# Decode attention with a Mish MLP: keys transposed by VectorE instead of TensorE, query and probabilities exchanged with keys and values as matmul operands, one load queue

## The chip, the cores and the metric

One core of one Trainium2 chip. A core has TensorE (matrix products from SBUF into PSUM), VectorE, ScalarE and GpSimd (element-wise work), SP (here it only issues DMAs), and 16 DMA engines between HBM and SBUF. SBUF and PSUM have 128 partitions. A matmul takes two operands: the *fixed* one (`lhsT`, up to 128x128) is loaded into the array by LDWEIGHTS, the *moving* one (`rhs`, up to 512 columns) is then streamed through. The metric is device time in microseconds (us), here the median of three runs: 239.27 us (238.69 to 239.35).

## The reference

One token for each of two batch rows goes through attention over a window of a key/value cache and, beside it, through a small MLP. With `x` of shape (2, 1, 448), 16 query heads, 8 key/value heads, head size 256 and a window of 4096 keys:

```
xn = layernorm(x)
q  = xn @ wq                                   # wq 448 x 4096, 16 heads of 256
k, v = k_cache[:, :, -4096:, :], v_cache[:, :, -4096:, :]   # (2, 8, 4096, 256), each for 2 query heads
p  = softmax(q . k / 16)                       # over 4096 keys
A  = (p . v) @ wo                              # wo 4096 x 448
h  = xn @ w1 + b1;  B = (h * tanh(softplus(h))) @ w2        # 448 -> 1792 -> 448
out = x + A + B
```

All arrays are bfloat16. The windows of the cache are 2 x 16 x 2 MB, 67.1 MB; wq and wo are 3.67 MB each, w1 and w2 1.61 MB each.

## The kernel before, in words

There are 16 *heads* in the loop: 8 key/value heads (`kvh`) times 2 batch rows (`b`). A head has 4096 keys, put on the partitions as 128 x 32: partition p holds keys 32p to 32p+31, in T = 32 blocks `t` of 128 keys, one key of each partition in a block.

For each `kvh` SP loads a slice of wq (lines 200 and 207) and of wo (line 213), and TensorE makes the transposed query `qT` (line 223). For each head SP loads the keys in two DMAs of 1 MB (`Kn`, line 241), and ScalarE's queue the values in two (`Vt`, line 245); each has three buffers of a whole head. Then:

- **Transposes** (`emit_transposes`): TensorE transposes a key block of 128x128 with the identity as moving operand (line 255, 64 per head), 8 blocks into one PSUM tile; VectorE copies five of the eight to SBUF (line 261), ScalarE three (line 265).
- **Scores** (`emit_scores`): each transposed block `KT` is loaded as the fixed operand and two columns, the two query heads, are streamed (line 274, 64 pairs of a load and a matmul per head). They run one group of 8 blocks behind the transposes.
- **Values**: ScalarE takes the exponential (line 289, 64 elements), VectorE the sums (line 292); then 32 matmuls with the probabilities (2 columns) as fixed operand and 256 value columns moving (line 301), a matmul for the denominators (line 308), the division (lines 316, 318), a transposition of the 2x256 result (lines 327, 332).
- After both batch rows of a `kvh`, four matmuls of 448 columns with wo add to `psA` (line 340).

The MLP's weights are loaded after `kvh` 1 (lines 98 to 105), and it is computed after `kvh` 3 (lines 149 to 189). At the end two additions (lines 354, 356) and the output DMA (line 357). Each engine runs its instructions in the order in which a scheduler has put them; the engines meet by semaphores. A DMA also waits for the one eight places before it, whose semaphore it reuses.

Of the kernel before, what the change touches and what calls it, by code (L numbers as in the profile page):

```python
# [12 lines left out]
FP32 = mybir.dt.float32  # L13


@with_exitstack
def kernel(
# [14 lines left out]
    P = 128  # L32

# [29 lines left out]
    wq_pool = ctx.enter_context(tc.tile_pool(name="wq", bufs=2))
    wo_pool = ctx.enter_context(tc.tile_pool(name="wo", bufs=2))
    qpool = ctx.enter_context(tc.tile_pool(name="q", bufs=2))
    kn_pool = ctx.enter_context(tc.tile_pool(name="kn", bufs=3))
    kt_pool = ctx.enter_context(tc.tile_pool(name="kt", bufs=2))
    v_pool = ctx.enter_context(tc.tile_pool(name="vv", bufs=3))
    pt_pool = ctx.enter_context(tc.tile_pool(name="pt", bufs=2))
    small = ctx.enter_context(tc.tile_pool(name="small", bufs=2))  # L70
    wmlp = ctx.enter_context(tc.tile_pool(name="wmlp", bufs=1))
    psum_tr = ctx.enter_context(tc.tile_pool(name="ps_tr", bufs=2, space=bass.MemoryType.PSUM))
    psum_sc = ctx.enter_context(tc.tile_pool(name="ps_sc", bufs=1, space=bass.MemoryType.PSUM))
    psum_po = ctx.enter_context(tc.tile_pool(name="ps_po", bufs=1, space=bass.MemoryType.PSUM))
    psum_ot = ctx.enter_context(tc.tile_pool(name="ps_ot", bufs=1, space=bass.MemoryType.PSUM))
    psum_mlp = ctx.enter_context(tc.tile_pool(name="ps_mlp", bufs=1, space=bass.MemoryType.PSUM))

    x_bf = consts.tile([Bsz, D], BF16)
    nc.sync.dma_start(out=x_bf[:, :], in_=A_x.flatten_outer_dims())

    ident = consts.tile([P, P], BF16)
    make_identity(nc, ident[:])

# [3 lines left out]
    ones1 = consts.tile([1, Bsz], BF16)  # L87
    nc.vector.memset(ones1[:], 1.0)

    ones_col = consts.tile([P, 1], FP32)  # L90
    nc.vector.memset(ones_col[:], 1.0)

    w1_sb = wmlp.tile([P, NJ, F], BF16)
    b1_sb = wmlp.tile([1, F], BF16)
    w2_sb = wmlp.tile([P, NFC, D], BF16)

    def emit_mlp_weight_dmas():
        nc.sync.dma_start(
            out=w1_sb[:, 0:nfull, :],
            in_=B_w1[0 : nfull * P, :].rearrange("(j p) n -> p j n", p=P),  # L100
        )
        if rem:
            nc.sync.dma_start(out=w1_sb[0:rem, nfull, :], in_=B_w1[nfull * P : D, :])
        nc.sync.dma_start(out=b1_sb[0:1, :], in_=B_b1.rearrange("(o f) -> o f", o=1))
        nc.sync.dma_start(
            out=w2_sb[:, :, :],
            in_=B_w2.rearrange("(c p) d -> p c d", p=P),
        )
# [18 lines left out]
    )  # L127

    xnT_ps = psum_misc.tile([P, NJ, Bsz], BF16, tag="pre")
    for j in range(NJ):  # L130
        csz = min(P, D - j * P)
        nc.tensor.transpose(  # L132
            xnT_ps[0:csz, j, :],
            xn_bf[0:Bsz, j * P : j * P + csz],
            ident[0:Bsz, 0:Bsz],
        )
    xnT_sb = consts.tile([P, NJ, Bsz], BF16)
    nc.vector.tensor_copy(out=xnT_sb[:, 0:nfull, :], in_=xnT_ps[:, 0:nfull, :])
# [3 lines left out]
    bsb = consts.tile([Bsz, D], FP32)

    def emit_mlp():
        hT_ps = psum_mlp.tile([P, NFC, Bsz], FP32, tag="m")
        for c in range(NFC):
            for j in range(NJ):
                ksz = min(P, D - j * P)
                nc.tensor.matmul(  # L149
                    hT_ps[:, c, :],  # L150
                    lhsT=w1_sb[0:ksz, j, c * P : (c + 1) * P],
                    rhs=xnT_sb[0:ksz, j, :],
                    start=(j == 0),
                    stop=False,
                )
            nc.tensor.matmul(  # L156
                hT_ps[:, c, :],
                lhsT=b1_sb[0:1, c * P : (c + 1) * P],
                rhs=ones1[0:1, 0:Bsz],
                start=False,  # L160
                stop=True,
            )
        h_sb = wmlp.tile([P, NFC, Bsz], FP32)
        nc.vector.tensor_copy(out=h_sb[:], in_=hT_ps[:])
        u_sb = wmlp.tile([P, NFC, Bsz], FP32)
        nc.scalar.activation(out=u_sb[:], in_=h_sb[:], func=ACT.Exp)
        v_sb = wmlp.tile([P, NFC, Bsz], FP32)
# [220 lines left out]
```

## Time and profile before

| | |
|---|---|
| median of three runs | 239.27 us |
| span of the profiled execution | 239.0 us |
| TensorE matmuls (PE), share of the span | 82%, 2872 instructions |
| TensorE weight loads (PEld) | 67% |
| VectorE (DVE) / ScalarE (ACT) | 33% / 28% |
| moved by DMA | 78.07 MB, 327 GB/s over the span |

The profiled execution is one run; its span, from the first to the last instruction, is 0.3 us short of the median time. PE and PEld overlap, and matmuls are pipelined: their busy time says that TensorE is at work, not that it is at its peak. In the chain of work that ended last TensorE has 57% of the span, DMA 20%, VectorE 11% and ScalarE 7%. The granted TensorE clock has two levels, 1.2 and 2.4 GHz; the profile gives it as a share of 2.4.

### The profile page before, as it was taken

To read this page: it belongs to the slowest core of one execution; us is meant where nothing else is said; L and a number is where in the kernel's file an instruction comes from. 1 tells how busy PE (TensorE), PEld (TensorE's weight loads), DVE (VectorE), ACT (ScalarE), POOL (GpSimd) and SP (SyncE) were. 2 spreads that over 40 slices of the span, in tenths; PEclk is the share of its full clock that TensorE was granted. 3 is DMA by queue.
4 is the path that set the end of the run, shared out by engine and by line. 5 is a ranking of instruction groups with operands and counts; after the bars stand their busy time and mean duration, and the time that the engine had idled before them with its cause. 6 is when DMAs were issued, how large, how long until landed. Compare 5 with 4: busy or idle time off the path is not lost.

```text
span 239.0 us, 6327 instructions
## 1 busy us (share of the span) xinstructions
PE 196.0 (82%) x2872; PEld 159.1 (67%) x2872; DVE 79.0 (33%) x217; ACT 67.2 (28%) x149; POOL 0.7 (0%) x6
## 2 busy tenths in 40 slices
PE   0228039949999999899989998999899989999892
PEld 0127037746797687778877877777777767777751
DVE  2003012411224253335333624352434334342603
ACT  2003104311113142315232523251425133432500
POOL 1000000000000000000000000000000000000000
PEclk9999999956857999999999999999999999999979
DMA  6999999999997999999999999999999999500000
GB/s 226 389 422 417 405 380 420 374 331 348 391 395 254 357 365 363 337 373 418 415 366 379 420 415 394 401 387 395 381 402 362 387 334 421 234 1 3 3 0 0
DMA packets 19605, 78.07 MB, mean 327 GB/s; under 512 B 1461, under 2 KB 10937, under 8 KB 11386
## 3 DMA queue, kind: packets, MB, share of 16 engines
q1 hardware_dynamic: 14970, 44.12, 48.9%
q10 hardware_dynamic: 4608, 33.56, 37.0%
q8 instruction: 22, 0.36, 0.6%
q14 instruction: 5, 0.04, 0.0%
HBM read 77.67 MB, written 0.00 MB: 325 GB/s over the span
## 4 chain that ended last, share of the span: by engine, by line
PE 57%; DMA 20%; DVE 11%; ACT 7%; issue 2%; SPq 1%; ACTq 0%
PE po L301 24%; PE pst L255 18%; DVE KT L261 9%; DMA wq_k<-in_A_wq_dram 7%; DMA w_sb<-in_B_w_dram 7%; ACT KT L265 7%; DMA Kn<-in_A_k_cache_dram 6%; PE psc L274 5%; PE psA L340 3%; PE qT_ps L223 3%; PE hT_ps L149 2%; DVE o_bf L318 1%; PE psB L182 1%; ACT pT L289 1%; PE hT_ps L156 1%
## 5 line engine op out<-in xcount | busy, mean ns | idle before, releaser
L265 ACT COPY KT<-pst 128x384 bf16<-128x384 bf16 x128 | 60.8, 478 | 150.6 <-DVE KT L261 117.5
L255 PE MATMUL pst<-ident,Kn 128*128 128x128 bf16 x1024 | 83.9, 233 | 9.9 <-DMA Kn<-in_A_k_cache_dram 5.6
L261 DVE COPY KT<-pst 128x640 bf16<-128x640 bf16 x128 | 61.8, 488 | 78.0 <-PE pst L255 76.1
L255 PEld LDWEIGHTS <-Kn 128*128 128x128 bf16 x1024 | 66.6, 104 | 11.0 <-DMA Kn<-in_A_k_cache_dram 5.7
L301 PE MATMUL po<-Vt,pT 128*2 128x256 bf16 x512 | 62.2, 283 | 1.1 <-ACT pT L289 0.7
L301 PEld LDWEIGHTS <-pT 128*2 128x2 bf16 x512 | 43.2, 87 | 17.7 <-ACT pT L289 2.4
L274 PE MATMUL psc<-qT_k,KT 128*128 128x2 bf16 x1024 | 49.5, 165 | 5.9 <-DVE KT L261 4.9
L274 PEld LDWEIGHTS <-KT 128*128 128x128 bf16 x1024 | 40.1, 98 | 16.7 <-DVE KT L261 10.2
L223 PE MATMUL qT_ps<-xnT_sb,wq_k 128*128 128x2 bf16 (+1 forms) x128 | 10.3, 170 | 14.3 <-DMA wq_k<-in_A_wq_dram 14.3
L316 DVE RECIPROCAL rec<-po 2x1 f32<-2x1 f32 x16 | 2.5, 155 | 57.1 <-PE po L308 57.1
L223 PEld LDWEIGHTS <-wq_k 128*128 128x128 bf16 (+1 forms) x128 | 8.3, 99 | 15.5 <-DMA wq_k<-in_A_wq_dram 14.6
L149 PE MATMUL hT_ps<-xnT_sb,w_sb 128*128 128x2 bf16 (+1 forms) x56 | 5.0, 172 | 3.5 <-DMA w_sb<-in_B_w_dram 3.5
L318 DVE TENSOR_SCALAR o_bf<-po,rec 2x256 bf16<-2x256 f32 x16 | 7.5, 471 | 0.5
L340 PE MATMUL psA<-wo_k,oT_k 128*2 128x448 bf16 x32 | 7.5, 355 | 0.3 <-DVE oT_k L332 0.3
L149 PEld LDWEIGHTS <-w_sb 128*128 128x128 bf16 (+1 forms) x56 | 3.5, 101 | 4.0 <-DMA w_sb<-in_B_w_dram 3.5
L289 ACT ACTIVATE pT<-psc 128x64 bf16<-128x64 f32 x16 | 3.6, 226 | 8.6 <-PE psc L274 4.7
L231 DVE CAST qT_k<-qT_ps 128x8 bf16<-128x8 f32 x8 | 1.3, 167 | 9.4 <-PE qT_ps L223 8.0
L292 DVE TENSOR_REDUCE red<-pT 128x2 f32<-128x64 bf16 x16 | 3.4, 210 | 2.3 <-ACT pT L289 2.3
L327 PE MATMUL oT_ps<-ident,o_bf 2*128 2x2 bf16 x32 | 3.2, 166 | 0.8 <-DVE o_bf L318 0.8
L132 PE MATMUL xnT_ps<-ident,xn_bf 2*128 2x2 bf16 (+1 forms) x4 | 0.4, 178 | 3.9 <-DVE xn_bf L120 3.9
L327 PEld LDWEIGHTS <-o_bf 2*128 2x128 bf16 x32 | 1.7, 92 | 2.7 <-DVE o_bf L318 0.9
L182 PE MATMUL psB<-w_sb,act_bf 128*2 128x448 bf16 x14 | 3.5, 352 | 0.0
(36 smaller groups left out, 23.8 us busy)
## 6 DMA issues: line engine op xcount, KB each, us to landing
Vt<-in_A_v_cache_dram ACTq DMA_DIRECT2D x32, 1024.0 KB, 7.8
Kn<-in_A_k_cache_dram SPq DMA_DIRECT2D x32, 1024.0 KB, 8.8
wo_k<-in_A_wo_dram SPq DMA_DIRECT2D x8, 448.0 KB, 9.2
wq_k<-in_A_wq_dram SPq DMA_DIRECT2D x8, 384.0 KB, 8.5
w_sb<-in_B_w_dram SPq DMA_DIRECT2D x1, 1568.0 KB, 20.4
w_sb<-in_B_w_dram SPq DMA_DIRECT2D x1, 1344.0 KB, 16.2
wq_k<-in_A_wq_dram SPq DMA_DIRECT2D x8, 64.0 KB, 8.3
w_sb<-in_B_w_dram SPq DMA_DIRECT2D x1, 224.0 KB, 17.0
```

The costliest lines, as they stand in the source:

```text
L149: nc.tensor.matmul(hT_ps[:, c, :], lhsT=w1_sb[0:ksz, j, c * P : (c + 1) * P], rhs=xnT_sb[0:ksz, j, :], start=(j == 0), stop=False,)
L182: nc.tensor.matmul(psB[:, :], lhsT=act_bf[:, c, :], rhs=w2_sb[:, c, :], start=(c == 0), stop=(c == NFC - 1),)
L223: nc.tensor.matmul(qT_ps[:, hl, dh, :], lhsT=wq_k[0:ksz, j, col0 : col0 + P], rhs=xnT_sb[0:ksz, j, :], start=(j == 0), stop=(j == NJ - 1),)
L255: nc.tensor.transpose(pst[:, tt, :], Kn[:, t, dh * P : (dh + 1) * P], ident[:],)
L261: nc.vector.tensor_copy(out=KT[:, dh, base : base + CSPLIT * P], in_=pst[:, 0:CSPLIT, :],)
L265: nc.scalar.copy(out=KT[:, dh, base + CSPLIT * P : base + GRP * P], in_=pst[:, CSPLIT:GRP, :],)
L274: nc.tensor.matmul(psc[:, t, :], lhsT=KT[:, dh, t * P : (t + 1) * P], rhs=qT_k[:, :, dh, b], start=(dh == 0), stop=(dh == NDH - 1),)
L289: nc.scalar.activation(out=pT[:], in_=psc[:], func=ACT.Exp, scale=scale)
L301: nc.tensor.matmul(po[:, 0:Dh], lhsT=pT[:, t, :], rhs=Vt[:, t, :], start=(t == 0), stop=(t == T - 1),)
L318: nc.vector.tensor_scalar(out=o_bf[:], in0=po[:, 0:Dh], scalar1=rec[:], scalar2=None, op0=ALU.mult,)
L327: nc.tensor.transpose(oT_ps[:, dh * rep : (dh + 1) * rep], o_bf[0:rep, dh * P : (dh + 1) * P], ident[0:rep, 0:rep],)
L340: nc.tensor.matmul(psA[:, :], lhsT=oT_k[:, :, col], rhs=wo_k[:, c, :], start=(kvh == 0 and hl == 0 and dh == 0), stop=(kvh == Hkv - 1 and ...
```

## The change

It is a new kernel for the same computation. A head is now worked on in two *steps* of 16 key blocks (`NH` = 2, 32 steps in all).

- **Loads.** All large loads are issued by SP in one order: the whole wq in two DMAs, then keys and values step by step, wo after the second batch row, w1 and w2 at step 3. wq and w1 lie on 112 partitions with four rows each, so that what a partition reads is 4 KB or more. Keys and values have six buffers each of half a head.
- **Keys** (`scores`): VectorE transposes the key tile in 32x32 blocks, with pairs of bf16 taken as one fp32 element (`kt`, 2048 elements a partition). A transposed tile then holds 32 elements of a key's head dimension on each 32 partitions, pairs side by side.
- **Scores**: the query is the fixed operand, block-diagonal over the four groups of 32 partitions (`qdiag`, eight matrices a head, written by GpSimd in `build_q`), and 512 columns of keys are moving, every second element (`ktv`); eight matmuls a step.
- **Probabilities**: ScalarE's exponential writes 512 columns and sums them as it goes; VectorE transposes them back in 32x32 blocks (`pT`).
- **Values** (`values`): a 128x128 block of values is the fixed operand (every second element of 256, `vv`), two columns of probabilities are moving; 32 pairs a step. The result is already transposed, so the transposition at the end of a head goes.
- wq is projected in two groups (`project`), the MLP in `dense_in` and `dense_out`; there is one addition at the end instead of two.

```diff
+    k_pool = ctx.enter_context(tc.tile_pool(name="kk", bufs=6))
+    v_pool = ctx.enter_context(tc.tile_pool(name="vv", bufs=6))
     kt_pool = ctx.enter_context(tc.tile_pool(name="kt", bufs=2))
+    p_pool = ctx.enter_context(tc.tile_pool(name="pp", bufs=2))
...
+        nc.sync.dma_start(
+            out=wq_sb[:, :, g * GW : (g + 1) * GW], in_=wq_in[:, :, g * GW : (g + 1) * GW]
+        )
...
+    def build_q(i):
+        kvh, b = heads[i]
+        t = qdiag[i % NW]
+        tv = t[:].rearrange("p (n e) c -> p n e c", e=NE)
+        for j in range(NQ):
+            rows = slice(j * Q, (j + 1) * Q)
+            for e in range(NE):
+                nc.gpsimd.tensor_copy(
+                    out=tv[rows, :, e, j * Q : j * Q + rep],
+                    in_=qrep[rows, :, kvh * rep : (kvh + 1) * rep, e, b],
+                )
...
+    def scores(s):
+        i = s // NH
+        kt = kt_pool.tile([P, TH * Dh], BF16, tag="kt", name="kt")
+        nc.vector.transpose(out=kt[:].bitcast(FP32), in_=k_t.pop(s)[:].bitcast(FP32))
+        ktv = kt[:].rearrange("p (t n c e) -> p n e t c", t=TH, n=NB, e=NE)
+        psc = ps_sc.tile([P, TH, Q], FP32, tag="sc", name="sc")
+        for n in range(NB):
+            for e in range(NE):
+                nc.tensor.matmul(
+                    psc[:],
+                    lhsT=qdiag[i % NW][:, n * NE + e, :],
+                    rhs=ktv[:, n, e, :, :],
...
+        nc.scalar.activation(
+            out=p_sb[:],
+            in_=psc[:].rearrange("p t c -> p (t c)"),
+            func=ACT.Exp,
+            scale=scale,
+            accum_out=state["rs", i][:, s % NH : s % NH + 1],
+        )
...
+    def values(s):
...
+        nc.vector.transpose(out=pT[:], in_=p_t.pop(s)[:])
...
+        vv = v[:].rearrange("p t (m c) -> p t c m", c=ND)
+        for t in range(TH):
+            for c in range(ND):
+                nc.tensor.matmul(
+                    po[:, c, :],
+                    lhsT=vv[:, t, c, :],
+                    rhs=pTv[:, t, 0:rep],
...
+        nc.vector.reciprocal(out=rec[:], in_=den[:])
...
+        nc.vector.tensor_tensor(
+            out=oT[:, :, :, b],
+            in0=po[:],
+            in1=rec[:].unsqueeze(1).to_broadcast([P, ND, rep]),
+            op=ALU.mult,
+        )
...
+    for s in range(NSTEP + 1):
+        if s + 2 < NSTEP:
+            load_k(s + 2)
+        if s + 1 < NSTEP:
+            load_v(s + 1)
...
+        if s < NSTEP:
+            scores(s)
+        if s >= 1:
+            values(s - 1)
```

VectorE before, in the second half of the program: a head's copies of the transposed keys (`KT<-pst`), the sum, the division and the small copy of the head before between them.

```order
L261 COPY KT_2243<-pst_2245 128x640 [waits PE_49]
L292 TENSOR_REDUCE red_2193<-pT_2191 128x2 [waits Activation_49]
L316 RECIPROCAL rec_2229<-po_2195 2x1 [waits PE_49]
L318 TENSOR_SCALAR o_bf_2231<-po_2195,rec_2229 2x256 [waits DVE_49]
L261 COPY KT_2243<-pst_2256 128x640 [waits PE_49]
L332 COPY oT_k_2030<-oT_ps_2233 128x4 [waits PE_49]
L261 COPY KT_2243<-pst_2267 128x640
```

VectorE after, at the same place: from the division of one head (`oT` from `o`) to that of the next. `kt<-k` is the transposition of a key tile, `pT<-p` that of the probabilities.

```order
L333 TENSOR_TENSOR oT_2008<-o_1908,rec_2006 128x4 [waits DVE_49,PE_49]
L299 STREAM_TRANSPOSE pT_2027<-p_1966 128x512 [waits Activation_49]
L271 STREAM_TRANSPOSE kt_2014<-k_1889 128x2048 [waits DMAHW1_49]
L271 STREAM_TRANSPOSE kt_2074<-k_1941 128x2048 [waits DMAHW3_49]
L299 STREAM_TRANSPOSE pT_2088<-p_2025 128x512 [waits Activation_49]
L329 RECIPROCAL rec_2125<-den_2122 128x2 [waits PE_49]
L333 TENSOR_TENSOR oT_2008<-o_2029,rec_2125 128x4 [waits DVE_49,PE_49]
```

The short copies that followed TensorE's transposes are gone. Two whole key tiles stand in a row, and the division of a head stands ahead of the next head's first `pT`.

TensorE after, at the same place: the denominator (`den`) behind the first value stage of a head, the scores of the next head (`sc_2076`), then the second value stage (`o_2029`, with 31 more pairs where the dots are), wo, and the scores of the step after.

```order
L321 MATMUL den_2122<-hsel_124,rs_1967 128x2 [waits Activation_49]
L276 LDWEIGHTS qdiag2_133 [waits DVE_49,Pool_49]
L276 MATMUL sc_2076<-kt_2074,qdiag2_133 128x512 [waits PE_49]
...
L308 LDWEIGHTS v_1943 [waits DMAHW4_49]
L308 MATMUL o_2029<-pT_2088,v_1943 128x2 [waits DVE_49]
...
L344 LDWEIGHTS oT_2008 [waits DVE_49]
...
L321 MATMUL den_2236<-hsel_124,rs_2086 128x2 [waits Activation_49]
L276 LDWEIGHTS qdiag2_133 [waits DVE_49]
L276 MATMUL sc_2138<-kt_2136,qdiag2_133 128x512 [waits PE_49]
```

A step's scores stand one step ahead of its values, and each waits for VectorE: the scores for `kt`, the values for `pT`.

## Rows read from the trace of the kernel before

**Rows 1.** The page: span, busy time, granted clock and GB/s in 40 slices.

```profile
span 239.0 us, 6327 instructions
...
PE 196.0 (82%) x2872; PEld 159.1 (67%) x2872; DVE 79.0 (33%) x217; ACT 67.2 (28%) x149; POOL 0.7 (0%) x6
...
PEclk9999999956857999999999999999999999999979
...
GB/s 226 389 422 417 405 380 420 374 331 348 391 395 254 357 365 363 337 373 418 415 366 379 420 415 394 401 387 395 381 402 362 387 334 421 234 1 3 3 0 0
```

**Rows 2.** Busy time by stretch: us, engines, granted clock, DMA share, GB/s.

```profile
0.00:6.00 6.00, 0.37 (x4) 0.28 (x4) 1.67 (x9) 1.58 (x2) 0.70 (x6) 1.00 0.70 226
132.00:144.00 12.00, 11.66 (x185) 9.24 (x183) 4.93 (x14) 4.43 (x10) 0.00 (x0) 1.00 1.02 418
```

**Rows 3.** DMA queues, 12 to 18 us: packets, MB, share of 16 engines.

```profile
DMA packets 480, 2.53 MB, mean 422 GB/s; under 512 B 58, under 2 KB 185, under 8 KB 185
...
q1 hardware_dynamic: 431, 2.26, 92.1%
```

**Rows 4.** DMA queues, 40 to 47 us.

```profile
DMA packets 605, 2.85 MB, mean 407 GB/s; under 512 B 41, under 2 KB 41, under 8 KB 427
```

**Rows 5.** DMA queues, 56 to 59 us.

```profile
DMA packets 1124, 1.03 MB, mean 342 GB/s; under 512 B 8, under 2 KB 1123, under 8 KB 1123
```

**Rows 6.** Waits of SP's queue: total us, times, longest.

```profile
SPq L241 <- PE pst L255: 62.2, 12, 10.0
```

**Rows 7.** Timeline of SP: start us, us, DMA issues.

```profile
123.73 12.09 SPq L241 DMA_DIRECT2D Kn<-in_A_k_cache_dram  x4
...
170.40 12.64 SPq L241 DMA_DIRECT2D Kn<-in_A_k_cache_dram  x4
```

**Rows 8.** Timeline of TensorE, ScalarE: pieces; start, us, instructions.

```profile
9.97 1.04 PE L223 MATMUL qT_ps<-xnT_sb,wq_k 64*128 64x2 bf16 x13 [1.49 <-DMA wq_k<-in_A_wq_dram]
...
16.59 1.89 PE L255 MATMUL pst<-ident,Kn 128*128 128x128 bf16 x16 [5.58 <-DMA Kn<-in_A_k_cache_dram]
...
205.94 0.23 ACT L289 ACTIVATE pT<-psc 128x64 bf16<-128x64 f32 x1
...
206.29 3.36 PEld L301 LDWEIGHTS <-pT 128*2 128x2 bf16 x32
206.29 3.65 PE L301 MATMUL po<-Vt,pT 128*2 128x256 bf16 x32
...
212.29 1.07 PE L255 MATMUL pst<-ident,Kn 128*128 128x128 bf16 x16
...
213.20 0.54 PE L274 MATMUL psc<-qT_k,KT 128*128 128x2 bf16 x16
```

**Rows 9.** Groups by line and shape: count, busy us, mean ns, idle before.

```profile
L265 ACT COPY KT<-pst 128x384 bf16<-128x384 bf16 x128 | 60.8, 478 | 150.6 <-DVE KT L261 117.5 <-PE pst L255 19.8 <-DMA Vt<-in_A_v_cache_dram 6.7
...
L318 DVE TENSOR_SCALAR o_bf<-po,rec 2x256 bf16<-2x256 f32 x16 | 7.5, 471 | 0.5
...
L292 DVE TENSOR_REDUCE red<-pT 128x2 f32<-128x64 bf16 x16 | 3.4, 210 | 2.3 <-ACT pT L289 2.3
...
L356 DVE TENSOR_TENSOR res<-fin,x_bf 2x448 bf16<-2x448 f32 x1 | 0.6, 614 | 0.0
```

**Rows 10.** Timeline of the end: start, us, instructions.

```profile
234.67 0.92 PE L340 MATMUL psA<-wo_k,oT_k 128*2 128x448 bf16 x4 [0.25 <-DVE oT_k L332]
235.62 0.61 DVE L354 TENSOR_TENSOR fin<-psA,bsb 2x448 f32<-2x448 f32 x1 [1.01 <-PE psA L340]
...
236.91 0.27 SPq L357 DMA_DIRECT2D out_dram<-res  x1
```

**Rows 11.** TensorE by the microsecond: us, busy (instructions), clock, DMA share, GB/s.

```profile
48.00:49.00 1.00, 1.00 (x13) 0.50 0.96 271
57.00:58.00 1.00, 1.00 (x8) 0.74 1.11 340
```

**Rows 12.** Timeline of TensorE from 54 us.

```profile
54.67 5.03 PE L301 MATMUL po<-Vt,pT 128*2 128x256 bf16 x32
```

More of the change, by code (lines that the diff above doesn't have):

```diff
@@ L81 @@
+    wq_sb = weights.tile([PD, NS, HqDh], BF16)
+    wq_in = A_wq.rearrange("(p s) n -> p s n", s=NS)
+    NG = 2
+    HG = Hq // NG
+    GW = HG * Dh
+    for g in range(NG):
+        nc.sync.dma_start(
+            out=wq_sb[:, :, g * GW : (g + 1) * GW], in_=wq_in[:, :, g * GW : (g + 1) * GW]
+        )
     ident = consts.tile([P, P], BF16)
     make_identity(nc, ident[:])
+    spread = consts.tile([P, NB, P], BF16)
+    nc.gpsimd.memset(spread[:], 0.0)
+    for b4 in range(NB):
+        rows = slice(b4 * Q, (b4 + 1) * Q)
+        for j in range(NQ):
+            nc.vector.tensor_copy(
+                out=spread[rows, b4, j * Q : (j + 1) * Q], in_=ident[rows, rows]
+            )
@@ L84 @@
+    hsel = consts.tile([P, rep], FP32)
+    nc.vector.tensor_copy(out=hsel[:], in_=ident[:, 0:rep])
+    for j in range(1, NQ):
+        nc.vector.tensor_tensor(
+            out=hsel[:], in0=hsel[:], in1=ident[:, j * Q : j * Q + rep], op=ALU.add
+        )
+    NW = 3
+    qdiag = []
+    for i in range(NW):
+        t = consts.tile([P, NB * NE, P], BF16, name=f"qdiag{i}")
+        nc.gpsimd.memset(t[:], 0.0)
+        qdiag.append(t)
     eps_t = consts.tile([Bsz, 1], FP32)
     nc.vector.memset(eps_t[:], 1e-5)
-    ones1 = consts.tile([1, Bsz], BF16)
@@ L142 @@
[L142 to L148, printed above, removed]
+    xnT_ps = ps_m.tile([P, NS, Bsz], BF16, tag="m", name="xnT_ps")
+    xn_v = xn_bf[:, :].rearrange("b (p s) -> b s p", s=NS)
+    for s in range(NS):
+        nc.tensor.transpose(xnT_ps[0:PD, s, :], xn_v[:, s, :], ident[0:Bsz, 0:Bsz])
+    xnT = consts.tile([PD, NS, Bsz], BF16)
@@ new lines, in dense_out, with load_k @@
+        nc.vector.tensor_tensor(out=xb[:], in0=psB[:, :], in1=x_bf[:], op=ALU.add)
+    NSTEP = len(heads) * NH
+    k_t, v_t, p_t, wo_t = {}, {}, {}, {}
+    psA = ps_a.tile([Bsz, D], FP32)
+    state = {}
+    def load_k(s):
+        i, half = divmod(s, NH)
+        kvh, b = heads[i]
+        t = k_pool.tile([P, TH * Dh], BF16, tag="k", name="k")
+        kin = A_k_cache[b, kvh, s0:Sk, :].rearrange("(p t) d -> p (t d)", p=P)
+        nc.sync.dma_start(out=t[:], in_=kin[:, half * TH * Dh : (half + 1) * TH * Dh])
+        k_t[s] = t
@@ L340 @@
                 nc.tensor.matmul(
                     psA[:, :],
[L342 to L354 removed]
+                    lhsT=oT[:, c, h, :],
```

394 lines of the change are left out of this document (162 added, 232 removed).

## The prediction

> **What bounds the kernel now.** I read the page first: TensorE is busy 82% of the span and nothing else over a third, and the line of GB/s stands near 400 until 206 us and at zero in the last 30 us [rows 1]. So loading is over long before the end, and TensorE is what runs on: the stages of nearly three heads fill those 30 us. The wait list of the load queue says the same of the time before: the key loads waited 62.2 us in total for TensorE's transposes, that is, for a free buffer [rows 6]. The queue's timeline gives the pace, a pair of heads every 23.3 us (123.73 to 147.06 to 170.40) [rows 7]. In such a pair 8.39 MB of keys and values and 0.46 MB of wo are read, 380 GB/s, where the stretches in which nothing holds the loads show more: 418 GB/s in 132 to 144 us [rows 2] and 422 in 12 to 18 us, there with one queue (q1) doing 92.1% of it [rows 3]. Small pieces are slower: 342 GB/s where nearly all packets are under 2 KB [rows 5], 407 where most lie between 2 and 8 KB [rows 4]. So TensorE is the bound; the same bytes at 418 GB/s would need 21.2 us a pair of heads, 2.1 less than it takes.
>
> **What the change removes.** TensorE loses its 1024 key transposes (16 in 1.07 us at full clock, 68 us in all) and the 1024 score pairs that load a key block as weights (16 in 0.54 us, 35 us); VectorE and ScalarE lose the copies of the transposes [rows 8, 9]. The value matmuls, 32 of 256 columns in 3.65 us per head (58 us), become 64 loads of values with two columns behind each.
>
> **What it adds, by the half head** (32 steps; one key and one value tile of 1.05 MB each).
> VectorE transposes 2048 elements a partition (kt) and 512 (pT). No transpose is in the trace. The reduction of 64 elements takes 210 ns, the addition of 448 takes 614 [rows 9]: 1.05 ns an element. By this kt is 0.21 + 1984 x 1.05 ns = 2.30 us and pT 0.68. The bounds: 0.78 ns an element from ScalarE's copy of 384 (a total of 1.6 us), and 1.84 from o_bf (471 ns for 256), 3.77 and 0.94 us [rows 9]. I take 2.30, since the shape of the 614 ns row is nearest in length.
> The Trainium skill ("VectorE: DVE Perf Modes", section "The three transpose paths") gives 311 ns for a VectorE transpose of 128x128 in bf16. An estimate by that figure alone is 2.43 ns an element, so 4.98 us for kt and 1.24 for pT; no run here shows it yet, and it is the last rival below.
> TensorE's scores are 8 matmuls of 512 columns. 32 of 256 columns take 3.65 us [rows 8], so one of 512 is 0.228 us and a step 1.82. At half clock 16 of 128 columns take 1.89 us [rows 8], so 0.47 and 3.78. The keys are read at every second element, which no row shows: the bounds are no loss, which I take, and double.
> The values are 32 pairs of a 128x128 weight load and two columns. The nearest pairs, 16 in 0.54 us [rows 8], make 34 ns each, 1.08 us a step. The wq pairs, 13 in 1.04 us, make 80 ns, 2.56 us; they alternate 128 and 64 rows, and the new loads have 128 but skip every second element. I take 1.08.
> ScalarE's exponential over 512 columns (0.64 us by 478 ns for 384 [rows 9]) lies beside the value matmuls of the step before. GpSimd writes eight small pieces of the query a head; its six instructions take 0.7 us in all [rows 1], so about 1 us a head, built a head ahead with three buffers. If that cover failed it would add at most this. The loads all go to SP, which has nothing else; the loads of values now stand behind key loads that wait for a buffer, but there are six of each, so the queue halts only when computing is over three steps behind.
>
> **The sum by loads.** Slice 0 to 6 us moved 226 GB/s x 6 = 1.36 MB [rows 2], which at 418 GB/s is 3.25 us: loads start, in effect, at 2.75. Keys and values, 67.1 MB at 418: 160.5. wq, w1 and w2, 6.88 MB now in rows of 4 KB and more, at 407 [rows 4]: 16.9. wo, 3.67 MB in 1.8 KB rows, between 342 and 407 GB/s (10.7 and 9.0): I take 9.8. The last byte lands at 190.0. The last value tile lands 1.2 us before it, with wo behind; its pairs (1.08) and the division (0.4) end 0.3 after wo; then four wo matmuls 0.92, one addition 0.61 where there were two, 2.09 from the output's issue to the end [rows 10], and three handovers of 0.12 (205.94 + 0.23 to 206.29 [rows 8]): 4.3. Together 194.3 us.
>
> **The sum by the engines.** VectorE runs in order, and in the new order a head's division stands ahead of the next pT, and behind this two kt in a row. So the engines don't overlap freely: the division of a head waits for its second value stage, which waits for the scores of the step after; then VectorE does pT and kt while TensorE waits. The loop over two steps is division 0.21, pT 0.68, kt 2.30, then scores, values, scores, values 2 x (1.82 + 1.08), with seven handovers of 0.12: 9.8 us, 4.9 a step. The loads need (2 x 1.05 MB at 418) + 0.3 of wo = 5.3. Neither leaves the other much. Ahead of the loop: wq has landed at 2.75 + 9.0 = 11.8, 128 pairs at 34 to 80 ns take 4.4 to 10.2, casts about 0.8, kt 2.3, so the first scores stand at 19 to 25; I take 23. The dense part holds TensorE once: 56 pairs at 80 ns 4.5, seven small operations of 0.2, 14 wo-like matmuls of 0.23: 9. So 23 + 9 + 32 x 4.9 + 4.3 = 193.1, at full clock.
> But the first stages don't get it: the transposes at 16.59 us took 1.89 us, those at 212.29 took 1.07 [rows 8] (the clock column reads 1.00 at both; the durations don't). I count three steps of scores at half clock, 3 x 1.96 = 5.9: 199.0, above the 194.3 of the loads. The profiled execution has a span of 239.0 and 0.3 around it to the median of 239.27. Forecast: 199 us.
>
> **Rivals.**
> 1. *TensorE falls to half clock again and again.* For it: at 48 us the granted clock was 0.50 (1.2 GHz) although TensorE was busy, with transposes and two-column pairs; it came back at 57 us under 256-column matmuls, begun at 54.67 [rows 11, 12]. In the new loop wide matmuls fill 3.6 us of 9.8; the rest is two-column pairs and waits. Against: the stages with 512 columns come twice in each loop, and half a clock makes TensorE busier. Each step so hit costs 1.96 us. Eight of 32: 208.8, near the end of the forecast's own range (194 to 210); sixteen: 224.5.
> The Trainium skill ("TensorE: Matmul & The Clock Gate", section "HAM oscillation — how this bites in real kernels") says that matmul bursts with longer waits for loads between them start cold each time. By that rule nearly all steps would be hit, toward the 256 us of the next rival; at 48 us the trace shows a fall without any wait, so it neither agrees nor disagrees on waits.
> 2. *Slower than before: the same mechanism, but in over 23 of the 32 steps.* (239 - 193.1)/1.96 = 23.4 is where it decides; all 32 give 256 us. Against: from 90 to 227 us the kernel before keeps its clock though 256-column matmuls fill only 31% of a head, 3.65 of 11.7 us [rows 1, 8].
> 3. *Reading every second element costs.* Weight loads at 80 ns: 4.9 + 1.48 a step, 240 us. Keys at double: 4.9 + 1.82, 251. For it: all weights and columns in the rows of before lie side by side, so no row excludes a price. Against: nothing but the least assumption.
> 4. *VectorE's transposes are slower.* At 1.84 ns an element the loop is 1.73 longer: 5.8 a step, 221 us.
> By the 311 ns of the page it would be 6.5 a step, 245 us; the rows at 1.05 ns speak against.
> 5. *The loads run slower than 418.* For it: a pair of heads shows 380 [rows 7]. Against: there the queue waited for buffers [rows 6], and one queue alone reached 422 [rows 3]. At 400 GB/s keys and values take 167.8 and the whole 202 us, at 380 it is 210: the upper end of the forecast's own range.
>
> **How the numbers follow.** The forecast with rival 5: 0.62. Rival 1 between 210 and 239: 0.18. Rival 4 at about 221: 0.07. Slower: rival 2 0.06, rival 3 0.04, rival 4 by the page's figure 0.02, together 0.12. No change to measure (within 0.3%) is 0.01; faster is 0.87. The range is 193 (loads without any loss in the engines) to 226 (rival 4, and rival 1 up to sixteen steps), which leaves out some 0.2.
>
> **What would show it.** Load share near full to 185 us or later, and 410 to 420 GB/s in the middle: the sum by loads is right. kt at 2.2 to 2.5 us: rival 4 is dead. Score matmuls at 0.22 us and a clock of 1.00 past 50 us: rival 1 is dead; at 0.45 it is alive. 32 value pairs in 1.1 us: rival 3 is dead. If VectorE's idle time before the division is put down to the value matmuls, and TensorE's before the scores to kt, the loop is as told. The forecast is wrong if loads end before 170 us in a faster kernel (then the rate was more than the rows show), or if SP waits for buffers through the middle (then the engines set the pace alone).

## The result, and the profile after

The changed kernel takes 212.0 us (median of four runs, 210.20 to 213.59) where the kernel before takes 239.3: the ratio is 0.885, with a 95% interval of 0.878 to 0.892. It is faster, inside the range of 193 to 226 us, and 13 us slower than the forecast of 199. The profiled execution took 213.59 us with a span of 211.8; the 1.8 us around the span are in the later runs of the kernel before as well (240.24 beside a span of 238.4), so they are no part of the change, though the forecast had only 0.3 for them. The ratios leave out runs that lie more than 1.5% above the fastest of their kernel, as the profiled run here does, and the medians keep them.

The page of the changed kernel, against [rows 1]: span, busy time, granted clock, DMA share and GB/s in 40 slices of 5.3 us.

```profile
span 211.8 us, 3784 instructions
...
PE 148.2 (70%) x1586; PEld 80.4 (38%) x1586; DVE 103.9 (49%) x134; ACT 25.1 (12%) x68; POOL 26.7 (13%) x138
...
PEclk9999997678555967696969797978888857696966
DMA  5999999999999999999999999999999999999500
GB/s 152 281 278 381 416 421 421 408 342 227 330 409 421 411 418 421 421 404 422 422 415 411 420 415 421 409 419 419 421 407 419 416 421 412 421 416 420 215 7 0
```

TensorE is down from 196 busy us to 148, and the DMA engines are busy to the last three slices, to 196 of 212 us, where the loads used to stop at 206 of 239. Two things are new: the clock row, full in [rows 1] but for six slices, now swings between 5 and 9 to the end; and the rate is low in two places, in the first three slices (152, 281, 278) and in those from 42 to 58 us (342, 227, 330).

The groups by line, as in [rows 9]: count, busy us, mean ns of one, idle time before and who ended it.

```profile
L276 PE MATMUL sc<-kt,qdiag 128*128 128x512 bf16 x256 | 91.0, 517 | 38.7 <-DVE kt L271 38.1
L271 DVE STREAM_TRANSPOSE kt<-k 128x2048 f32<-128x2048 f32 x32 | 72.8, 2285 | 10.3 <-DMA k<-in_A_k_cache_dram 10.1
...
L299 DVE STREAM_TRANSPOSE pT<-p 128x512 bf16<-128x512 bf16 x32 | 22.5, 704 | 31.6 <-ACT p L286 31.6
...
L333 DVE TENSOR_TENSOR oT<-o,rec 128x4 bf16<-128x4 f32 x16 | 2.6, 165 | 38.5 <-PE o L308 38.5
```

The transposes came out as worked out: 2285 ns for kt (2.30) and 704 for pT (0.68). The Trainium skill ("VectorE: DVE Perf Modes", "The three transpose paths") gives 311 ns for 128x128 in bf16. A straight line through the two durations here, if a 4-byte element costs what a 2-byte one does, is 1.03 ns an element of a partition and 177 ns beside it; by it 128 elements would take 309 ns, an estimate. So the trace agrees with the page's figure as far as it goes, and what fails is the prediction's use of it, 2.43 ns for every element: it spread the fixed part over 128 elements. The scores' mean of 517 ns is over twice the 0.228 us expected.

The timeline of two steps in the middle: start us, us, engine, line, instructions, in brackets the wait before and who ended it.

```profile
147.11 3.48 PE L276 MATMUL sc<-kt,qdiag 128*128 128x512 bf16 x8 [1.58 <-DVE kt L271]
...
151.61 1.89 PE L276 MATMUL sc<-kt,qdiag 128*128 128x512 bf16 x8
...
154.32 0.17 DVE L333 TENSOR_TENSOR oT<-o,rec 128x4 bf16<-128x4 f32 x1 [2.20 <-PE o L308]
154.40 0.70 DVE L299 STREAM_TRANSPOSE pT<-p 128x512 bf16<-128x512 bf16 x1
155.02 2.27 DVE L271 STREAM_TRANSPOSE kt<-k 128x2048 f32<-128x2048 f32 x1
...
157.35 3.48 PE L276 MATMUL sc<-kt,qdiag 128*128 128x512 bf16 x8 [2.69 <-DVE kt L271]
```

Here the loop can be read as it was told: the division (oT) waits 2.20 us for the second values, then pT and kt run while TensorE waits 2.69 us. One round is 157.35 - 147.11 = 10.24 us. And it shows what was not counted: the eight matmuls behind that wait take 3.48 us, the next eight, which have no wait before them, 1.89. Of the 30 score stages after the first two, 19 take 2.6 to 3.6 us in this run, whose mean clock of 0.80 is the lowest of the four (the others have 0.81 to 0.83). The 32 value pairs take 0.94 us, less than the 1.08 expected: reading every second element costs next to nothing in keys (1.89 us for eight matmuls of 512 columns, where 1.82 was expected) or values.

TensorE, clock and GB/s by stretch: us, busy (instructions) of PE, PEld, DVE, ACT and POOL, granted clock, DMA share, GB/s.

```profile
6.00:12.00 6.00, 0.18 (x1) 0.10 (x1) 0.80 (x7) 0.00 (x0) 0.00 (x0) 1.00 1.04 277
12.00:18.00 6.00, 0.47 (x17) 0.47 (x18) 0.00 (x0) 0.00 (x0) 0.00 (x0) 1.00 1.02 297
48.00:54.00 6.00, 4.16 (x45) 2.12 (x44) 2.98 (x3) 0.69 (x2) 0.00 (x0) 0.78 0.99 234
```

The middle moves 404 to 422 GB/s (the page above), as forecast. But wq, which was to run at 407, moved at 277 to 297, and the stretch of w1 and w2 at 234. None of this is a wait for a free buffer: all waits of SP's key and value loads are for earlier transfers, these two foremost (total us, times, longest).

```profile
SPq L249 <- DMA v<-in_A_v_cache_dram: 55.8, 25, 3.7
SPq L257 <- DMA k<-in_A_k_cache_dram: 44.1, 21, 2.2
```

The end: the loads thin out at 198 us, the last bytes move at about 203 (first line: PE, PEld, DVE, ACT, POOL, clock, DMA share, GB/s).

```profile
202.00:203.00 1.00, 1.00 (x4) 0.38 (x3) 0.00 (x0) 0.00 (x0) 0.00 (x0) 0.50 0.05 20
...
198.62 0.17 DVE L333 TENSOR_TENSOR oT<-o,rec 128x4 bf16<-128x4 f32 x1 [2.21 <-PE o L308]
198.70 0.70 DVE L299 STREAM_TRANSPOSE pT<-p 128x512 bf16<-128x512 bf16 x1
199.32 2.27 DVE L271 STREAM_TRANSPOSE kt<-k 128x2048 f32<-128x2048 f32 x1
...
201.65 3.52 PE L276 MATMUL sc<-kt,qdiag 128*128 128x512 bf16 x8 [2.69 <-DVE kt L271]
...
207.88 1.21 PE L344 MATMUL psA<-wo,oT 128*2 128x448 bf16 x4 [0.26 <-DVE oT L333]
...
209.77 0.32 SPq L380 DMA_DIRECT2D out_dram<-res  x1
```

The last key tile had landed, but its transpose stands behind the division and a pT on VectorE, so it starts at 199.32; then the half-clock scores (3.52), and the wo matmuls (1.21 against 0.92 in [rows 10]) follow. From 199.3 to the end of the span are 12.5 us.

### The profile page after: what moved, and what is told of

It reads as the page before. It is cut to its first block, busy times and chain, and to the rows that moved or that the text cites. A ratio compares the mean times of both kernels' runs of the same rounds, so it can differ in the third digit from the quotient of the medians.

```text
span 211.8 us, 3784 instructions
## 1 busy us (share of the span) xinstructions
PE 148.2 (70%) x1586; PEld 80.4 (38%) x1586; DVE 103.9 (49%) x134; ACT 25.1 (12%) x68; POOL 26.7 (13%) x138
## 4 chain that ended last, share of the span: by engine, by line
DMA 64%; PE 24%; DVE 9%; issue 1%; ACT 0%; SPq 0%; ACTq 0%
DMA k<-in_A_k_cache_dram 30%; DMA v<-in_A_v_cache_dram 29%; PE sc L276 15%; DVE kt L271 6%; DMA wq_sb<-in_A_wq_dram 5%; PE o L308 4%; PE psB L229 3%; DVE pT L299 2%; PE den L321 1%; PE psA L344 1%; DVE oT L333 0%; DVE res L379 0%; ACT p L286 0%; SPq L249 0%; DVE den_sb L222 0%
## 5 line engine op out<-in xcount | busy, mean ns | idle before, releaser
L276 PE MATMUL sc<-kt,qdiag 128*128 128x512 bf16 x256 | 91.0, 517 | 38.7 <-DVE kt L271 38.1
L271 DVE STREAM_TRANSPOSE kt<-k 128x2048 f32<-128x2048 f32 x32 | 72.8, 2285 | 10.3 <-DMA k<-in_A_k_cache_dram 10.1
L276 PEld LDWEIGHTS <-qdiag 128*128 128x128 bf16 x256 | 29.3, 123 | 82.4 <-issue 38.1
L178 POOL COPY qdiag<-qrep 32x8 bf16<-32x8 bf16 x128 | 22.9, 184 | 146.3 <-PE sc L276 116.2
L286 ACT ACTIVATE p<-sc 128x512 bf16<-128x512 f32 x32 | 19.1, 597 | 174.0 <-PE sc L276 174.0
L299 DVE STREAM_TRANSPOSE pT<-p 128x512 bf16<-128x512 bf16 x32 | 22.5, 704 | 31.6 <-ACT p L286 31.6
L308 PEld LDWEIGHTS <-v 128*128 128x128 bf16 x1024 | 31.7, 99 | 13.3 <-issue 10.3
L308 PE MATMUL o<-pT,v 128*128 128x2 bf16 x1024 | 30.6, 164 | 0.4 <-DVE rec L329 0.4
L321 PE MATMUL den<-hsel,rs 128*128 128x2 f32 x64 | 12.9, 273 | 0.1
L321 PEld LDWEIGHTS den<-hsel,rs 128*128 128x128 f32 x64 | 10.2, 202 | 4.6 <-issue 2.7
```

The source lines that it names most:

```text
L178: nc.gpsimd.tensor_copy(out=tv[rows, :, e, j * Q : j * Q + rep], in_=qrep[rows, :, kvh * rep : (kvh + 1) * rep, e, b],)
L271: nc.vector.transpose(out=kt[:].bitcast(FP32), in_=k_t.pop(s)[:].bitcast(FP32))
L276: nc.tensor.matmul(psc[:], lhsT=qdiag[i % NW][:, n * NE + e, :], rhs=ktv[:, n, e, :, :], start=(n == 0 and e == 0), stop=(n == NB - 1 and ...
L286: nc.scalar.activation(out=p_sb[:], in_=psc[:].rearrange("p t c -> p (t c)"), func=ACT.Exp, scale=scale, accum_out=state["rs", i][:, s % N ...
L299: nc.vector.transpose(out=pT[:], in_=p_t.pop(s)[:])
L308: nc.tensor.matmul(po[:, c, :], lhsT=vv[:, t, c, :], rhs=pTv[:, t, 0:rep], start=(half == 0 and t == 0 and c == 0), stop=(half == NH - 1 a ...
```

## The experiments

The theory after this reading: the time is set by two chains that are nearly equal, the loads (late because wq and w1 lie on 112 partitions) and the engines' loop (long because its order makes TensorE wait and the wait brings half clock). The rivals: only the loads, only the order, only the clock, or the loads held up by the engines.

**Loads alone.** All loads of the changed kernel in its order; no projection, scores, values or dense part.

```
-    project(0)
...
-            scores(s)
...
-            values(s - 1)
...
-            dense_out()
...
+    nc.vector.tensor_tensor(out=res[:], in0=w[0:Bsz, 0, 0:D], in1=x_bf[:], op=ALU.add)
```

> Leaves out everything but the loads, which stand in the changed kernel's order on the same queue; the output is x plus the last tile of wo. The question is whether the 9.5 us by which the loads end later than forecast (199.5 us in the changed kernel, 190.0 in the sum) come from the transfers themselves or from the engines that work beside them. Theory A (the transfers: wq and w1, which lie on 112 partitions, run at some 250 to 290 GB/s wherever they stand): the loads still end at 196 to 200 us, wq takes 13 to 14 us as in the changed kernel, and the stretch of w1 and w2 shows 220 to 300 GB/s. Rival B (the engines and their buffers hold the loads up): the loads end at 188 to 192 us and wq runs at 400 GB/s or more.

201.13 us. Its stretches (columns as above):

```profile
6.00:12.00 6.00, 0.00 (x0) 0.00 (x0) 0.75 (x6) 0.00 (x0) 0.00 (x0) 1.00 1.05 273
12.00:18.00 6.00, 0.00 (x0) 0.00 (x0) 0.00 (x0) 0.00 (x0) 0.00 (x0) 1.00 1.03 291
48.00:54.00 6.00, 0.00 (x0) 0.00 (x0) 0.00 (x0) 0.00 (x0) 0.00 (x0) 1.00 1.00 323
```

wq is as slow as in the whole kernel, with nothing beside it: theory A, and the rival that engines hold it up falls for wq. The last tile of wo is read as it lands:

```profile
196.91 0.38 DVE L365 TENSOR_TENSOR res<-wo,x_bf 2x448 bf16<-2x448 bf16 x1 [190.07 <-DMA wo<-in_A_wo_dram]
```

So the transfers alone end 7 us later than the forecast's 190.0. In the stretch of w1 theory A is only half right: 323 GB/s where the whole kernel has 234. How much that costs shows in SP's issues, since each large load goes out when the one eight places before it has landed: the key load that waits for w2, and the last tile of wo, in the whole kernel and then in the loads alone (start us).

```profile
61.38 0.33 SPq L249 DMA_DIRECT2D k<-in_A_k_cache_dram  x1
184.73 0.38 SPq L262 DMA_DIRECT2D wo<-in_A_wo_dram  x1
...
56.34 0.33 SPq L249 DMA_DIRECT2D k<-in_A_k_cache_dram  x1
178.27 0.38 SPq L262 DMA_DIRECT2D wo<-in_A_wo_dram  x1
```

With the engines running the loads are 5.0 us late when w2 has landed, 1.3 of them from before this stretch (the key load at 26.32 us went out at 25.01 alone), and 6.5 at the end (about 203 us for 196.9); why the engines slow the loads, no run here settles.

**Shapes of transfers.** Loads only, each behind the one before.

```
+    nc.sync.dma_start(out=big[0:PD, 0:16384], in_=wq_f)      # wq, 112 rows of 32 KB
+    nc.sync.dma_start(out=big[:, 0:14336], in_=wq_flat)      # the same bytes, 128 of 28 KB
...
+    for n in (128, 112, 96, 64):
+        nc.sync.dma_start(out=big[0:n, 0:8192], in_=kin[0:n, :])
```

> Leaves out everything but loads of several shapes, one after another into one tile, so that each waits until the one before has landed; the output is x plus what landed last. Theory A (fewer than 128 partitions make a transfer slow): wq and w1 on 112 partitions at 250 to 290 GB/s whatever the piece, on 128 partitions in one row (28 and 12 KB) at 380 to 420 GB/s; keys of 16 KB on 112 partitions at 260 to 300, on 128 at 400 or more. Rival B (the size of a piece, 4 KB in wq): wq in rows of 32 KB on 112 partitions at 400, keys in pieces of 4 KB on 128 partitions at 250 to 300. Rival C (where wq and w1 lie in memory): both slow in every shape, keys fast in every shape. All rates are read from the first packet of a transfer to its landing; each has about 2 us of start in it, so a transfer of 1.8 MB shows some 300 GB/s at best and one of 3.7 MB some 350.

The issues on SP (start us); each goes out when the one before has landed.

```profile
19.62 0.37 SPq L94 DMA_DIRECT2D big<-in_A_wq_dram  x1
35.89 0.36 SPq L96 DMA_DIRECT2D big<-in_A_wq_dram  x1
47.00 0.32 SPq L98 DMA_DIRECT2D big<-in_B_w_dram  x1
54.68 0.35 SPq L99 DMA_DIRECT2D big<-in_B_w_dram  x1
61.01 27.08 SPq L102 DMA_DIRECT2D big<-in_A_k_cache_dram  x4
```

wq on 112 partitions took 35.89 - 19.62 = 16.27 us, the same 3.67 MB on 128 took 11.11; less the 2.0 us that even the output's 1.8 KB need from issue to end, 257 and 403 GB/s. w1 the same way: 283 and 371. And keys, where only the number of partitions changes, by the microsecond (us, clock, DMA share, GB/s at the end of a row), on 128 (first row), 112 and 96 partitions:

```profile
66.00:67.00 1.00, 0.00 (x0) 0.00 (x0) 1.00 0.95 410
72.00:73.00 1.00, 0.00 (x0) 0.00 (x0) 1.00 1.03 246
82.00:83.00 1.00, 0.00 (x0) 0.00 (x0) 1.00 1.05 246
```

410 GB/s on 128 partitions, about 250 on 112 and 96, with the DMA engines as busy (share about 1). The rate varies from one microsecond to the next; whole transfers, from issue to issue less the 2.0 us, make 369, 234, 223, and 200 on 64 partitions. So it is the number of partitions: rival B falls (32 KB rows were slow too) and rival C as well (keys were slow too). The keys in pieces of 4 KB took 6.3 us for 1.05 MB on 128 partitions, too short to tell their rate from the start.

**Weights on 128 partitions, in the kernel.**

```
-    wq_in = A_wq.rearrange("(p s) n -> p s n", s=NS)               # 112 partitions, NS = 4
+    wq_in = A_wq[0:DM, :].rearrange("(p s) n -> p s n", s=NM)      # 128 partitions, NM = 3
+    nc.sync.dma_start(out=wqr_sb[:], in_=A_wq[DM:D, :].rearrange("p (h n) -> (p h) n", h=2))
-        nc.sync.dma_start(out=w1_sb[:], in_=B_w1.rearrange("(p s) n -> p s n", s=NS))
+        nc.sync.dma_start(out=w1_sb[:], in_=B_w1[0:DM, :].rearrange("(p s) n -> p s n", s=NM))
+        nc.sync.dma_start(out=w1r_sb[:], in_=B_w1[DM:D, :])
```

> Nothing left out. The changed kernel with wq and w1 on 128 partitions: rows 0 to 383 as three rows to a partition, the 64 rows of wq that are left as half rows on 128 partitions (with the input spread to match), the 64 of w1 on 64 partitions. The order of everything else is that of the changed kernel. Theory A (112 partitions cost the rate, and the loads bind with the loop beside them): wq takes 9 to 10 us instead of 13.5 to 14, w1 and w2 some 2 us less, the loads end at 192 to 195 instead of 199.5, and the time is 204 to 207.5 us. Rival B (the loop of the engines sets the end alone, at 10.3 us for two steps): the loads end early, but the time follows only what the earlier first scores give, 207.5 to 210. Rival C (the rate in the kernel does not follow the partitions): loads end at 197 to 200, the time is 210 to 213.

Ratio 0.858 (0.851 to 0.865), so 6.4 us less than the changed kernel's 0.885 on the 239.3 us of before. The medians of all four runs differ less, 208.0 and 212.0, so the gain is 4 to 6.4 us. wq's last half is there at 13.4 us instead of 17.5, and the loads thin out at 191 instead of 198. But their end no longer meets the kernel's: the last transpose of keys still stands behind the division, at 192.88, and the end comes 12.5 us later at 205.4. The seventh score stage starts at 65.63 us instead of 68.47 and the last at 195.21 instead of 201.65: 2.8 us come from an earlier start, 3.6 from rounds that no longer wait for keys. So the time lies between the two theories (the median is in B's range, the profiled 207.2 in A's), and the engines' loop now sets the end alone, as in B.

**Engines alone, twice.** Key and value loads end with the sixth step; later steps use those tiles again.

```
     def load_k(s):
...
+        if s >= 6:
+            k_t[s] = k_t0[s % 6]
+            return
```

> Leaves out the loads of keys and values from the seventh step on; later steps compute on the first six tiles again, so the engines do all the work of the changed kernel, in its order, and never wait for a load after the start. Theory A (the loop of division, transposes, scores and values binds by itself, half clock included): a pair of steps takes 10.2 to 10.4 us as in the last pairs of the changed kernel, the clock is about 0.8, and the time is 200 to 204 us. Rival B (the loop is as forecast, 9.8 us for two steps, and only waits for loads keep the clock low): clock 0.95 or more, time 190 to 195 us. Rival C (the engines run far ahead when they may): 180 us or less.

153.66 us, in the range of rival C, but it doesn't show what C says of the changed kernel: without the later loads the scheduler put transposes of keys further ahead, so this was not the changed kernel's order. What it does show is the floor of the engines: with one more transpose ahead, four steps took 12.4 us (TensorE's first scores of every second pair of steps):

```profile
112.41 0.38 PE L283 MATMUL sc<-kt,qdiag 128*128 128x512 bf16 x1
...
124.85 0.38 PE L283 MATMUL sc<-kt,qdiag 128*128 128x512 bf16 x1
```

6.2 us for two steps is what VectorE needs: 2 x (2.28 + 0.69) + 0.13 + 0.16 = 6.23. So I ran it again with the changed kernel's order written by hand.

> Leaves out the loads of keys and values from the seventh step on (later steps compute on the first six tiles again), as the kernel of the engines alone did; but the order of VectorE and TensorE is now written by hand and is the changed kernel's: two transposes of keys, probabilities, division, output product, probabilities. In the earlier one the scheduler had put other transposes of keys ahead, and it took 153.66 us. Theory A (the changed kernel's order makes a loop that binds by itself): a pair of steps takes 10.2 to 10.4 us with the first score stage of each pair at 3.5 us, the whole 195 to 203 us. Rival B (the loop binds, but only waits for loads let the clock fall): a pair takes 8.7 us with all score stages at 1.9, the whole 170 to 177 us. Rival C (the order alone binds nothing): a pair takes 7.5 us or less, the whole 150 to 160 us.

209.51 us, longer than any theory said, and all but the whole kernel's time. The round is the one of theory A, 10.24 us each time (timeline, then TensorE's clock by the microsecond):

```profile
125.67 3.41 PE L295 MATMUL sc<-kt,qdiag 128*128 128x512 bf16 x8 [1.90 <-DVE kt L286]
...
130.17 1.90 PE L295 MATMUL sc<-kt,qdiag 128*128 128x512 bf16 x8
...
133.58 4.46 DVE L286 STREAM_TRANSPOSE kt<-k 128x2048 f32<-128x2048 f32 x2
...
135.91 3.41 PE L295 MATMUL sc<-kt,qdiag 128*128 128x512 bf16 x8 [3.07 <-DVE kt L286]
```

```profile
134.00:135.00 1.00, 0.00 (x0) 0.00 (x0) 1.00 (x1) 0.00 (x0) 0.00 (x0) 1.00 0.00 0
136.00:137.00 1.00, 1.00 (x3) 0.33 (x4) 1.00 (x1) 0.00 (x0) 0.00 (x0) 0.50 0.00 0
139.00:140.00 1.00, 1.00 (x35) 0.86 (x33) 0.00 (x0) 0.64 (x2) 0.62 (x4) 1.00 0.00 0
```

What the expectation had too low is the stretch ahead: with the first rounds and the dense part the eighth score stage starts at 74.56 us, and 12 rounds and an end of 10.3 follow. So the engines, in this order and with the wait for wq ahead of the first scores, need 209.5 us by themselves, and the loads 201.1: the changed kernel, at 212.0, is bound by the loop, with the loads close behind.

**Half clock by itself.** Eight more matmuls that nobody reads, in TensorE's wait: first in the kernel of the engines alone, in the changed kernel's order.

```
+        for n in range(8):
+            nc.tensor.matmul(
+                fill[:], lhsT=wq_sb[:, 0, 0:P], rhs=wq_sb[:, 0, 0:512], start=True, stop=True
+            )
...
+            do_val(s + 1)
+            do_fill()
+            do_oT(i)
```

> As the kernel before it (loads left out from the seventh step on, the changed kernel's order by hand), with the eight dummy matmuls of 512 columns after each head's last values. Theory A (half clock is in the loop because TensorE waits 2.7 us in each pair): the clock goes to 0.95 or more and a pair from 10.3 to 8.6 to 9.0 us, the whole to 172 to 180 us. Rival B (the dummies only take the place of the wait): the clock rises, the pair stays at 10 us or more.

189.45 us, clock 0.98, a round of 8.73 us: theory A's clock and round, but not its 172 to 180 us, since the eighth score stage again starts late, at 73.02:

```profile
122.20 1.89 PE L354 MATMUL fill<-wq_sb 112*128 112x512 bf16 x8
...
125.41 1.91 PE L296 MATMUL sc<-kt,qdiag 128*128 128x512 bf16 x8 [1.32 <-DVE kt L287]
...
134.14 1.91 PE L296 MATMUL sc<-kt,qdiag 128*128 128x512 bf16 x8 [0.47 <-DVE kt L287]
```

The stage behind the wait now takes 1.91 us instead of 3.41, and 209.5 - 189.5 = 20 us is the price of half clock in this order with the loads left out (some 13 rounds by 1.5). Then with all loads in place, and the control without the dummies:

> Nothing left out. The order of VectorE and TensorE is that of the changed kernel, written by hand (only the projections of the second half of wq stand before the first scores), and after each head's last values TensorE gets eight more matmuls of 512 columns on wq into a bank of their own, whose result nobody reads: 1.8 us at full clock, in the stretch of about 2.7 us in which TensorE waits for the second of two transposes of keys. Theory A (the wait lets the clock fall, and the first score stage of each pair of steps then takes 3.5 us instead of 1.9): the mean clock rises from 0.80 to 0.95 or more, every score stage takes 1.9 to 2.1 us, the tail after the last load gets 1.6 to 2.5 us shorter, and the time is 206 to 210 us, since the loads' end at 199.5 stays. Rival B (the clock does not follow these waits): the clock stays at 0.8 and the time at 212 to 216. Rival C (the fillers stand in the way of the scores): the clock rises, the pair of steps does not get shorter than 10.3 us, the time is 211 to 214.

> Nothing left out: the changed kernel's order of VectorE and TensorE written by hand, without the dummy matmuls; the control for the kernel that had them. Theory A (the dummies had kept the clock and shortened the tail): the clock is 0.80 to 0.83 and the time 1.5 to 4 us longer than the 211.72 us with them, 213 to 216. Rival B (with the loads in place the dummies change nothing that ends late): 210 to 213 us at a clock of 0.80 to 0.83.

With the dummies the ratio is 0.882 (0.875 to 0.889), without them 0.880 (0.874 to 0.886): no difference, though the clock is 0.89 to 0.93 with them and 0.82 to 0.85 without. Of the second expectation rival B holds. Of the first none holds whole: the clock rises, but less than theory A said, and the time (211.72) is rival C's without its reason, since a round that doesn't wait for keys takes 8.74 us (45.01 to 53.75). That fits the two floors: with the loop at 189 us alone, the loads set the end; in the profile with the dummies VectorE waits 22.6 us for key loads where the control has 10.0, and 8 us of the span stand behind the last load.

**The order.** One transpose of keys a step, the division one step later.

```
+                do_kt(s)
+                do_sc(s)
+            if s >= 3 and s % NH == 1:
+                do_rec(s // NH - 1)
+                do_oT(s // NH - 1)
+                do_psa(s // NH - 1)
+            if s >= 1:
+                do_pT(s - 1)
+                do_val(s - 1)
```

> Nothing left out. Written order on VectorE and TensorE: one transpose of keys in each step, then the probabilities of the step before; the head's division and output product stand one step later; scores, then values of the step before on TensorE. Theory A (the tail of 12.2 us instead of 4.3, and the wait of 2.7 us on TensorE in every second step, come from two transposes of keys standing together ahead of the second half's probabilities): no wait of TensorE for keys over 1 us in the last half of the run, a step by the engines alone of 4.6 to 4.9 us, the loads still end at 198 to 200, the tail is 5.5 to 8.5 us, the time 205 to 208.5 us. Rival B (the tail is the half clock alone, and the order only moves the wait): the waits are spread over both steps, the clock stays at 0.8 or falls, the time is 210 to 215. Rival C (the loads hold all): the engines run at the loads' pace with waits for keys from the loads, the tail goes to 5 us or less, and the time is 203 to 206.

Ratio 0.872 (0.867 to 0.877), 3 us less than the changed kernel; 209.86 us, slower than theory A said, at rival B's clock (0.79 to 0.81). VectorE now waits 68.7 us for key loads where it was 10.1 (count, busy us, mean ns, idle time before and who ended it):

```profile
L279 DVE STREAM_TRANSPOSE kt<-k 128x2048 f32<-128x2048 f32 x32 | 73.7, 2306 | 68.7 <-DMA k<-in_A_k_cache_dram 68.7
```

So the loads bind, as rival C has it, but the tail did not go to 5 us: the last keys reach VectorE at 195.8 and the end is at 209.1, with the last scores (2.67 us) and the wo matmuls (1.65) still slowed by the clock. None of the three holds whole.

**Both, and a shorter end.** Weights on 128 partitions, that order, the last keys and the last wo tile loaded before the last values, the last denominator before the last values.

```
+    KEND = [("k", n) for n in range(NSTEP - 3, NSTEP)]
...
+            if s == NSTEP:
+                do_den(s // NH - 1)
+            if s >= 1:
+                do_pT(s - 1)
```

> Nothing left out. The weights on 128 partitions, the written order of one transpose of keys a step with the division one step later, the last three key tiles and the last tile of wo loaded ahead of the last values, and the last head's denominator ahead of its last values. Theory A (loads bind, and the tail is the chain behind the last load): loads end at 190 to 193, the tail behind them is 5 to 7.5 us, the time 197.5 to 202 us. Rival B (half clock in the tail keeps the chain at 9 us or more, or the ring that finishes last is late): 202 to 205. Rival C (the loads end no earlier): 205 to 209.

201.67 us (201.16 to 201.91), ratio 0.840 (0.837 to 0.843): faster than both kernels, theory A. It changes four things at once; how much each gives, no run separates. The end of it:

```profile
194.48 0.95 PE L362 MATMUL o<-pT,v 128*128 128x2 bf16 x32 [1.30 <-DMA v<-in_A_v_cache_dram]
...
195.69 0.92 PE L410 MATMUL psA<-wo,oT 128*2 128x448 bf16 x4 [0.26 <-DVE oT L394]
...
197.28 0.32 SPq L491 DMA_DIRECT2D out_dram<-res  x1
```

Now the last values wait for their load (1.30 us, to 194.48), and from there to the end of the span are 4.9 us: the 4.3 us chain of the forecast, found once nothing else stands in front of it. The clock is still 0.81, but VectorE waits 60.7 us for key loads, and these cover it.

> Nothing left out. As the kernel before it, with six dummy matmuls of 512 columns after the values of each of the last steps and one such group before the last denominator, so that TensorE keeps its clock in the tail. Theory A: the last scores take 1.9 us and the last four matmuls with wo 0.92, the tail is 1 to 2 us shorter than without them, the time 0.5 to 2 us less. Rival B (the dummies delay the chain as much as the clock gives): no difference within 0.3%.

Ratio 0.849 (0.845 to 0.853), 1.5 us slower than without the dummies: rival B and worse, since eleven dummies (2.97 us) ran between the last exponential and the last denominator. There was nothing to gain: without them the last scores (1.89 us) and the wo matmuls (0.92) were at full clock already.

## Why the prediction was right in sign and range, and 13 us short

- *VectorE's durations, values, strided reads, loads in the middle*: as forecast (kt 2.285 us for 2.30, pT 0.70 for 0.68, 32 value pairs 0.94 for 1.08, 404 to 422 GB/s). Rivals 3 and 4 are out, and rival 5 for the middle. What bounds the kernel before was read from its trace; no run tests it.
- *The sum by the engines* failed at "I count three steps of scores at half clock". It was 19 of 30, one in nearly every round: rival 1, given 0.18, and the time lies in its 210 to 239 us. A round at full clock is 8.73 us and not 9.8, and half clock adds 1.5 and not 1.96, so a round is 10.24 us; both sizes were too large, which is why the 19 stages gave 212 us where rival 1 had 224.5 for sixteen. By the prediction's own sizes nineteen make 193.1 + 19 x 1.96 = 230.3 us, above its range: that the time fell inside is in part luck, two sizes too large against a count too small. Set against the sum, the span of the profiled run is 12.8 us longer (211.8 for 199.0). The eighth score stage starts 2.0 us late (74.2, where 23 + 9 + 7 x 4.9 + 5.9 is 72.2): the first scores came at 24.76 for 23, the dense part held TensorE 10.6 us (57.85 to 68.47) for 9. The 12 rounds to the last scores took 127.4 us (74.2 to 201.65) for 12 x 9.8 = 117.6: of these 9.8 us more, 5.3 are a round's 10.24, half clock included, for the forecast's 9.8, and 4.5 lie in rounds that also waited for loads. The end from the last scores took 10.2 for 9.2 (4.9 + 4.3).
- *The argument against rival 1*, that half a clock keeps TensorE busier, missed that in the steady rounds the clock is low only behind the wait: 1.00 while TensorE waits, 0.50 (1.2 GHz) when the scores begin, 1.00 again three us later. The Trainium skill ("TensorE: Matmul & The Clock Gate", "HAM oscillation — how this bites in real kernels") says that bursts of matmuls with longer waits for loads between them start cold each time. The trace agrees for the stage behind the wait of 1.6 to 2.7 us, here for VectorE. The second stage of a round follows on without idle time and is at full clock (1.89 us), so it is not "nearly all steps", as the prediction read the rule, but one in two.
- *The sum by loads* failed at "6.88 MB now in rows of 4 KB and more, at 407". The term looked at the size of a piece; the number of partitions was what had changed, from 128 to 112, and it costs 257 against 403 GB/s. Alone, the last byte lands at 196.9 us for 190.0, and in the kernel at about 203; there the weights' layout is worth 4 to 6.4 us.
- *That the larger of two sums is the time* nearly held for this kernel, with the right sums: 201.1 us for the loads alone and 209.5 for the engines alone make 212.0 together. It is no rule: with the dummies 201.1 and 189.5 make 211.7, since the loads run late beside the engines and work stands behind the last of them.

## What to carry to other kernels

Write the in-order loop of an engine that feeds TensorE as a round, find the wait in it, and ask from the trace's clock whether the matmuls behind that wait pay half clock, as here; then ask whether one operation moved ahead of the wait (here a key transpose before the division) takes both away. When a change regroups a weight for longer rows, check that the transfer still fills all 128 partitions. And before a cure is tried on one of two chains, run each alone: the dummies gave 20 us to the engines alone, and nothing to the kernel with all its loads.

## What the runs showed of the hardware

- A transfer to 112 or 96 partitions moves about 250 GB/s where the same one to 128 moves some 400 (wq 257 and 403; key rows 246 and 410), and the DMA engines show as busy in both.
- A weight load of 128x128 with two columns behind takes 29 ns a pair in a run of 32 (0.94 us), 0.95 to 1.03 at half clock: it does not follow the clock, as the 512-column matmuls do (0.24 and 0.44 us).
- In the stretch of w1 and w2 the loads moved 323 GB/s alone and 234 with the engines running, and by its end they were 5.0 us behind, 1.3 of them from before; why stays open.
